# The first five attention steps of a banded-attention and FFN kernel: mask and maximum by one VectorE instruction per head pair, in place in the PSUM bank, and a new table of order constants for the beginning

## The chip, the cores and the metric

One NeuronCore of one Trainium2 chip runs the whole program. The metric is the device time of one execution in microseconds (us). Three timed runs of the kernel before gave 839.41, 840.69 and 839.26 us; the median is 839.41 us. Everything that is said of engines comes from one further, profiled execution.

## The reference

Attention over 8 sequences of 576 tokens with 8 heads of 64, each query seeing itself and the 63 keys ahead of it, and a feed-forward layer on the result. Cut to what matters:

```python
scores = scale * (q @ k.T)                       # scale = 1/8
mask = (rel >= 0) & (rel < 64)                   # rel = query position - key position
scores = where(mask, scores, -1e9)
attn = exp(scores - max(scores));  attn /= sum(attn) + 1e-9
x = (attn @ v)  as  [4608 tokens, 512]
h = x @ w_in                                     # 512 -> 2048
g = h if h >= 1;  0 if h <= -1;  (h + 1)**2 / 4 between
out = g @ w_out                                  # 2048 -> 512
```

All is float32. The kernel gets float32 accuracy out of a faster matmul format by splitting each operand into a high part (rounded to that format, `fp32r`) and a low part (the rest), and adding three products of parts.

## The kernel before

**Tiles and steps.** The tokens are cut into 9 tiles of 512, and an attention step handles 128 tokens of all 8 heads, so a tile takes four steps: 0 to 3 for tile 0, 4 to 7 for tile 1. Tiles 0, 1 and 2 go through the FFN plainly: for each of 16 slices f of the 2048 hidden columns, 12 matmuls of `ffn_in` (L1153, called IN below), the gate (`ffn_relu` L1163 on ACT, the square L1168 on ACT or L1170 on DVE, `ffn_gate` L1175 on DVE), the split into high and low (`ffn_high` L1180 on ACT, `ffn_low` L1185), and 12 matmuls of `ffn_out` (L1199, called OUT). In tile 0 the slices 0 to 2 go in two halves of 256 tokens (12 IN, 6 OUT each, f0h0 being the first half of slice 0). The last six tiles go in pairs by a scheme with fewer products (L928, L1014).

**Weights.** All weights are loaded once, as 64-bit integers that hold float32 values, and each slice is made into a high and a low part by seven operations: ACT `w_rest` (L342, tile u) and `w_sign` (L319, tile raw); DVE two limits (L323), a shift (L335) and `w_join` (L346); ACT `w_high` (L290, into wts); DVE `w_low` (L358). The slices 0 to 3 come in two units of 128x512 elements (8 units), the slices 4 to 15 in one of 128x1024.

**A step of attention.** `att_scores` (L439) multiplies q and k into two PSUM banks, one for each half of the heads. The steps 0 to 3 add the mask on PE: ahead of the scores, a matmul of an identity with a rounded mask (L432) is put into each bank; the identity and the mask are rounded by two ACT instructions (`round_masks`, L423 and L424). Then DVE takes the maximum over each row (L473), scales it (L475), ACT takes the exponentials out of the bank with their sums (L486, eight instructions a step), DVE inverts the sums (L493, L494) and multiplies (L501), PE transposes (L537), ACT or DVE copies the transposed block out (L290, L292, tile ptd), PE multiplies by v (L552), and the result is split into the high and low parts xh (L290 or L292) and xl (L565) that the FFN reads. Step 4 masks on DVE instead: L469 multiplies by the scale, adds the mask and writes sm in SBUF, L473 takes the maximum of it, and the exponentials read sm. From step 5 on (`s >= SOON`) another form is used: one DVE instruction per head, `tensor_tensor_reduce` (L462, two rows in the profile: CUSTOM_DVE and a short READ_ACCUMULATOR), adds the mask and takes the maximum, and a transposition through DRAM takes the place of PE's.

**What sets the order.** `Plan` (L128) is a list scheduler that runs while the program is built: each piece of work has a key, a cost for each engine that may take it, the pieces it depends on and the buffers it takes and gives back. It picks the next piece by when it could start and by its key. The engines' queues are then fixed, and each engine works its own queue in order and waits where an operand is not there. The constants at the head of the file (A_FIRST, W_FIRST, W_LATE, D_LATE, G_LATE and so on) are shifts of those keys. DMAs are issued from SP's queue in the plan's order too, but for the first k and the first unit of weights, which ACT's queue issues.

Of the kernel before, what the change touches and what calls it, by code (L numbers as in the profile page):

```python
# [20 lines left out]
P = 128  # L21
# [15 lines left out]
PE_MASKS = 4  # L37
# [15 lines left out]
V_LATE = 2.92  # L53
W0_KEY = -100.2
FIRST_LOAD = 0, (0,)
M_LATE = 1
W0_STEP = 12.29
FINE = 4
NWARM = 8
A_FIRST = (-102.6, -95.58, -95.43, -95)  # L60
A_NEXT = 1.57
A_STEP = 4.75
A_SPAN = 2.18
A_LEAD = 4.64
O_LAG = 2.79
# [33 lines left out]
V_LATE_2 = 14.69  # L99
# [119 lines left out]
def banded_attention_then_ffn(ctx: ExitStack, tc: tile.TileContext, q, k, v, w, masks, out, out_t, dims):  # L219
# [30 lines left out]
    idr = const.tile([P, P], F32R, name="idr")  # L250
    mskr = const.tile([P, 2, WIN], F32R, name="mskr")
# [170 lines left out]
    def round_masks():  # L422
        nc.scalar.copy(idr, idt)  # L423
        nc.scalar.mul(mskr, msk[:, :2], 1.0 / scale)  # L424

    def att_scores(s, masked, pool):
        qt, kt = qts.pop(s), kts.pop(s)
        banks = [banks_of_heads(pool) for _ in range(2)]
        if masked:
            m = mskr[:, variant(s), :].unsqueeze(1).broadcast_to([P, NP, WIN])  # L430
            for ps in banks:
                nc.tensor.matmul(ps.rearrange("p a n -> p (a n)"), lhsT=idr, rhs=m, start=True, stop=False)  # L432
        m, n = (SQ, NEAR) if near(s) else (QB, WIN)
        for p in range(NP):
            for i in range(SB // m):
                r = slice(i * m, (i + 1) * m)
                o = rows_of(i // 2, i % 2) if near(s) else r
                for h in range(2):
                    nc.tensor.matmul(  # L439
                        banks[h][o, p, :n], lhsT=qt[half[h], p, r], rhs=kt[half[h], p, i * m:i * m + n],  # L440
                        start=not masked, stop=not masked or p == NP - 1,
                    )
# [12 lines left out]
    def att_masked(s, h):  # L455
# [11 lines left out]
        m = nmsk[:, variant(s), :NEAR] if near(s) else msk[:, variant(s)]  # L467
        m = m.unsqueeze(1).broadcast_to(sm.shape)
        nc.vector.scalar_tensor_tensor(out=sm, in0=ps, scalar=scale, in1=m, op0=ALU.mult, op1=ALU.add)  # L469

    def att_max(s, h, masked):
        ps, sm, nm, _ = blk[s, h]
        nc.vector.tensor_reduce(out=nm, in_=ps if masked else sm, axis=AX.X, op=ALU.max, negate=True)  # L473
        if masked:
            nc.vector.tensor_scalar_mul(nm, nm, scale)  # L475

    def att_exp(s, h, masked):
# [190 lines left out]
    def add_step(t, i):  # L668
# [3 lines left out]
        masked = s < PE_MASKS  # L672
# [23 lines left out]
        needs = [xq, xk] + [last["r"]] * masked + last["s"]  # L696
        if before and (t < PLAIN or len(before) == BEHIND):
# [4 lines left out]
            def do(e):  # L702
                att_scores(s, masked, ps)
# [7 lines left out]
        else:  # L711
            xs = add(
                key, dict(PE=S_PE[near(s)] + 500 * masked), lambda e: att_scores(s, masked, ps), needs,
# [713 lines left out]
```

## Time and profile before

| | |
|---|---|
| three timed runs | 839.41, 840.69, 839.26 us |
| the profiled execution | 843.4 us |
| its span, from the first instruction to the last | 841.6 us |
| mean granted TensorE clock | 0.994 |
| PE busy | 821.6 us (98%) |
| DVE busy | 687.0 us (82%) |
| ACT busy | 533.5 us (63%) |
| POOL busy | 213.8 us (25%) |

The profiled execution took 1.8 us more than its span, and 4.0 us more than the median of the timed runs. In a list of groups, a row holds the line, engine, operation, output<-input, shapes and count, then busy time and mean duration in ns, then the idle time ahead of the group and what ended it. In a timeline a row is start, duration, engine, line and shapes, with the idle time ahead of it in brackets. Rows of one engine overlap: the next instruction starts a little before the row of the last one ends, so what an instruction costs in a full queue is the distance between starts. PE rows of small float32 matmuls come in twos per instruction (16 score matmuls are 32 records).

### The profile page before, as it was taken

What the parts mean: (1) busy time and instruction counts of PE and PEld (TensorE: products, weight loads), DVE (VectorE), ACT (ScalarE), POOL (GpSimd) and SP (SyncE); (2) the same over time, 40 slices, a digit from 0 to 9 for tenths busy, and PEclk for the clock granted to TensorE, in tenths of its full rate; (3) what the DMA queues carried; (4) which work ended last, traced back from release to release, by engine and by line L of the source; (5) the groups of instructions that cost most, each with busy time, mean ns of one, the idle gap of its engine ahead of it and who ended that gap; (6) DMA issues with size and microseconds to landing.
All of it is one profiled execution on the core that took longest, in us unless ns stands there. A gap on an engine that the chain in (4) does not pass through costs nothing.

```text
span 841.6 us, 18582 instructions
## 1 busy us (share of the span) xinstructions
PE 821.6 (98%) x6588; PEld 672.1 (80%) x6588; DVE 687.0 (82%) x1613; ACT 533.5 (63%) x1303; POOL 213.8 (25%) x226
## 2 busy tenths in 40 slices
PE   7889999999999999999999999999999999999998
PEld 5767788878787878788888888888888888888886
DVE  6999996468757789888899986888999848878964
ACT  5999983545654764756775654777756536566442
POOL 1000014335664636221233320122332201100100
PEclk8999999999999999999999999999999999999999
DMA  8994359996788797788898898888888877777775
GB/s 322 394 375 170 100 165 331 362 331 200 214 265 262 219 285 235 271 252 272 272 333 253 284 316 281 269 268 282 302 252 244 294 230 198 192 195 193 198 224 164
DMA packets 151901, 216.08 MB, mean 257 GB/s; under 512 B 11904, under 2 KB 75264, under 8 KB 151808
## 3 DMA queue, kind: packets, MB, share of 16 engines
q1 hardware_dynamic: 151520, 213.97, 80.2%
q8 instruction: 53, 0.87, 0.4%
q10 hardware_dynamic: 288, 0.92, 0.3%
q14 instruction: 40, 0.33, 0.1%
HBM read 163.72 MB, written 51.12 MB: 255 GB/s over the span
## 4 chain that ended last, share of the span: by engine, by line
PE 75%; DVE 10%; DMA 7%; ACT 3%; issue 2%; POOL 2%; SPq 1%; ACTq 0%; POOLq 0%; DVEq 0%
PE acc L1014 27%; PE ps_h L928 14%; PE acc L928 14%; PE ps_h L1153 8%; PE acc L1199 7%; DMA kept<-u 4%; PE ps_a L439 2%; DVE u L842 1%; PE ps_a L552 1%; DVE u L857 1%; PE ps_h L552 1%; DVE u L849 1%; DMA raw<-in_w 1%; DVE wts L358 1%; DMA kt<-in_k 1%
## 5 line engine op out<-in xcount | busy, mean ns | idle before, releaser
L1014 PE MATMUL acc<-op,wts 128*128 128x512 f32 x576 | 137.7, 390 | 0.0
L1153 PE MATMUL ps_h<-xh,wts 128*128 128x512 f32 (+1 forms) x424 | 131.2, 376 | 6.1 <-DVE a L1175 4.4
L290 ACT CAST op<-g 128x512 fp32r<-128x512 f32 x129 | 80.2, 622 | 77.4 <-PE acc L1014 49.3
L1014 PEld LDWEIGHTS acc<-op,wts 128*128 128x128 f32 x576 | 107.8, 188 | 22.5
L1199 PE MATMUL acc<-wts,gh 128*128 128x512 f32 x384 | 120.1, 394 | 0.7 <-ACT gh L1180 0.7
L482 ACT ACTIVATE sm<-sm,nm 128x96 f32<-128x96 f32 x248 | 89.5, 363 | 12.3 <-DVE nm L462 11.6
L1153 PEld LDWEIGHTS ps_h<-xh,wts 128*128 128x128 f32 x424 | 78.0, 190 | 22.6 <-DVE a L1175 6.5
L1005 DVE TENSOR_TENSOR op<-g,op 128x512 fp32r<-128x512 f32 x107 | 76.7, 718 | 20.7 <-ACT op L290 20.2
L928 PE MATMUL ps_h<-wts 128*128 128x512 f32 x360 | 92.0, 391 | 0.0
L928 PE MATMUL acc<-wts 128*128 128x512 f32 x360 | 91.5, 389 | 0.0
L1199 PEld LDWEIGHTS acc<-wts,gh 128*128 128x128 f32 x384 | 70.8, 188 | 16.0 <-ACT gh L1180 1.1
L1168 ACT ACTIVATE a<-a 128x512 f32<-128x512 f32 (+1 forms) x125 | 77.1, 617 | 3.8
L1153 PE MATMUL ps_h<-xl,wts 128*128 128x512 f32 (+1 forms) x212 | 78.8, 372 | 0.6 <-DVE xl L565 0.6
L928 PEld LDWEIGHTS acc<-wts 128*128 128x128 f32 x360 | 67.5, 188 | 14.2
L928 PEld LDWEIGHTS ps_h<-wts 128*128 128x128 f32 x360 | 67.2, 188 | 14.2
L1199 PE MATMUL acc<-wts,gl 128*128 128x512 f32 x192 | 75.3, 392 | 1.4 <-DVE gl L1185 1.4
L1163 ACT ACTIVATE a<-g 128x512 f32<-128x512 f32 x96 | 60.5, 630 | 19.4 <-DVE g L943 14.0
L1175 DVE SCALAR_TENSOR_TENSOR g<-a,g 128x512 f32<-128x512 f32 x96 | 68.1, 716 | 3.8 <-ACT a L1168 3.2
L1005 POOL TENSOR_TENSOR op<-g,op 128x512 fp32r<-128x512 f32 x28 | 36.1, 1295 | 129.5 <-ACT op L290 118.1
L1185 POOL TENSOR_TENSOR gl<-a,gh 128x512 fp32r<-128x512 f32 (+1 forms) x34 | 48.6, 1429 | 45.0 <-ACT gh L1180 43.2
L992 DVE TENSOR_TENSOR g<-g 128x512 f32<-128x512 f32 x83 | 58.4, 717 | 0.5
L1175 DVE SCALAR_TENSOR_TENSOR a<-a,ps_h 128x512 f32<-128x512 f32 (+1 forms) x53 | 33.3, 628 | 25.1 <-ACT a L1168 24.9
(145 smaller groups left out, 1544.5 us busy)
## 6 DMA issues: line engine op xcount, KB each, us to landing
wts<-kept SPq DMA_DIRECT2D x240, 256.0 KB, 3.6
vt<-in_v SPq DMA_DIRECT2D x72, 256.0 KB, 4.9
ptd<-moved SPq DMA_DIRECT2D x31, 512.0 KB, 4.7
kt<-in_k SPq DMA_DIRECT2D x35, 384.0 KB, 5.1
kept<-wts SPq DMA_DIRECT2D x48, 256.0 KB, 4.8
gh<-kept SPq DMA_DIRECT2D x48, 256.0 KB, 3.7
gl<-kept SPq DMA_DIRECT2D x48, 256.0 KB, 3.6
raw<-in_w SPq DMA_DIRECT2D x12, 1023.8 KB, 10.6
```

The lines of the kernel that those rows point to most:

```text
L290: nc.scalar.copy(dst, src)
L482: nc.scalar.activation(t, t, AF.Exp, bias=nm[:, g:g + 1], scale=-1.0, accum_out=den[:, g:g + 1])
L928: nc.tensor.matmul(ps, lhsT=r[:, part, cp], rhs=x_op(k, xp)[:, cp], start=j in (0, 1, 3, 4) and i == 0 and cp == 0, stop=j in (1, 2, 5, 6) ...
L992: engine[eng].tensor_tensor(out=g[:, out], in0=g[:, a], in1=g[:, b], op=op)
L1005: engine[eng].tensor_tensor(out=low, in0=g_of(n)[:, of], in1=high.bitcast(F32), op=ALU.subtract)
L1014: nc.tensor.matmul(opened[b][m], lhsT=r[:, part, m], rhs=op[xp], start=j in (0, 1, 3, 4) and i == 0 and n == 0, stop=j in (1, 2, 5, 6) and ...
L1153: nc.tensor.matmul(ps, lhsT=wts[f, 0][:, part, c * P:(c + 1) * P], rhs=x[:, c, r], start=(c == 0 and j == 0), stop=(c == NP - 1 and j == 2),)
L1163: nc.scalar.activation(gs[t, f, r.start][0], phs[t, f, r.start], AF.Relu, bias=0.5, scale=0.5)
L1168: nc.scalar.activation(a, a, AF.Square)
L1175: nc.vector.scalar_tensor_tensor(out=ps if t >= PLAIN else a, in0=a, scalar=1.0, in1=ps, op0=ALU.min, op1=ALU.max)
L1185: engine[eng].tensor_tensor(out=g[2], in0=g[0], in1=g[1].bitcast(F32), op=ALU.subtract)
L1199: nc.tensor.matmul(acc[t, i][:, n], lhsT=g[:, sub], rhs=wts[f, 1][:, part, n], start=(q == 0 and j == 0), stop=(q == NF - 1 and j == 2 and ...
```

## The change

The steps 0 to 4 now mask as the later steps do: for each of the four heads of a bank one `tensor_tensor_reduce` adds the mask to the negated, scaled scores, writes the result back into the bank where it stood, and leaves the minimum in nm. The exponentials read the bank (with scale -1), for step 4 too. The mask matmuls, `round_masks`, the two rounded tiles, the separate maximum and its scaling are gone. The rest of the diff is constants: those of the beginning (A_FIRST, the new A_SHIFT, W_FIRST with a value for each of 14 slices, W_LATE, D_LATE, L_LEAD_1, B_DUE_1, O_LAG_1 for tile 0) and, by small amounts, those of the later stages.

```diff
-PE_MASKS = 4
-A_FIRST = (-102.6, -95.58, -95.43, -95)
+A_FIRST = (-102.4, -117.29, -54.2, -100.65)
+A_SHIFT = (0.68, 0.08, 0.09, 3.56, 0.35, 0.89, -2.62, 0.86)
...
-    def round_masks():
-        nc.scalar.copy(idr, idt)
-        nc.scalar.mul(mskr, msk[:, :2], 1.0 / scale)
-
-    def att_scores(s, masked, pool):
+    def att_scores(s, pool):
         qt, kt = qts.pop(s), kts.pop(s)
         banks = [banks_of_heads(pool) for _ in range(2)]
-        if masked:
-            m = mskr[:, variant(s), :].unsqueeze(1).broadcast_to([P, NP, WIN])
-            for ps in banks:
-                nc.tensor.matmul(ps.rearrange("p a n -> p (a n)"), lhsT=idr, rhs=m, start=True, stop=False)
...
-        m = nmsk[:, variant(s), :NEAR] if near(s) else msk[:, variant(s)]
-        m = m.unsqueeze(1).broadcast_to(sm.shape)
-        nc.vector.scalar_tensor_tensor(out=sm, in0=ps, scalar=scale, in1=m, op0=ALU.mult, op1=ALU.add)
-
-    def att_max(s, h, masked):
-        ps, sm, nm, _ = blk[s, h]
-        nc.vector.tensor_reduce(out=nm, in_=ps if masked else sm, axis=AX.X, op=ALU.max, negate=True)
-        if masked:
-            nc.vector.tensor_scalar_mul(nm, nm, scale)
+        nm = blk[s, h][2]
+        for p in range(NP):
+            nc.vector.tensor_tensor_reduce(
+                out=ps[:, p], in0=ps[:, p], in1=msk[:, variant(s)], scale=-scale,
+                scalar=3.0e38, op0=ALU.add, op1=ALU.min, accum_out=nm[:, p:p + 1],
+            )
...
         for p in range(NP):
             nc.scalar.activation(
-                sm[:, p, :], (ps if masked else sm)[:, p, :], AF.Exp, bias=nm[:, p:p + 1],
-                scale=scale if masked else 1.0, accum_out=den[:, p:p + 1],
+                sm[:, p, :], ps[:, p, :], AF.Exp, bias=nm[:, p:p + 1], scale=-1.0, accum_out=den[:, p:p + 1],
             )
```

What moves is seen best in the queues. ACT's queue from its first compute instruction on, before: u, raw and wts are the three weight operations, `sm,den` the exponentials of steps 0 (out of ps_a) and 1 (out of acc), ptd a transposed block that is copied out.

```order
6 L342 ACTIVATE u<-raw 128x512
7 L319 ACTIVATE raw<-raw 128x512
8 L486 ACTIVATE sm,den<-ps_a,nm 128x128 x8
9 L290 CAST wts<-u 128x512
10 L342 ACTIVATE u<-raw 128x512
11 L290 COPY ptd<-ps_h 128x512
12 L486 ACTIVATE sm,den<-acc,nm 128x128 x8
13 L319 ACTIVATE raw<-raw 128x512
14 L342 ACTIVATE u<-raw 128x512
15 L319 ACTIVATE raw<-raw 128x512
16 L290 CAST xh<-acc 128x4x128
```

The same stretch of ACT's queue now (lines are shifted by the edit: L341, L318 and L289 are the weight operations, L474 the exponentials).

```order
4 L341 ACTIVATE u<-raw 128x512
5 L318 ACTIVATE raw<-raw 128x512
6 L341 ACTIVATE u<-raw 128x512
7 L318 ACTIVATE raw<-raw 128x512
8 L289 CAST wts<-u 128x512 x2
9 L341 ACTIVATE u<-raw 128x512
10 L318 ACTIVATE raw<-raw 128x512
11 L341 ACTIVATE u<-raw 128x512
12 L289 CAST wts<-u 128x512
13 L318 ACTIVATE raw<-raw 128x512
14 L474 ACTIVATE sm,den<-ps_a,nm 128x128 x8
15 L474 ACTIVATE sm,den<-acc,nm 128x128 x8
```

Four units of weights now stand ahead of the first exponential where one stood; ahead of the first gate (row 22 before, row 29 now) stand six first and second weight operations in place of three, five third ones in place of two, and two xh in place of one, while the exponentials of the steps 0 to 3 and the copies there are the same. SP's queue follows: it now begins with a unit of weights and has six of them ahead of the q of step 2, where it had one.

PE's queue before, from the scores of step 0 on: L432 are the mask matmuls, L439 scores, L537 transposes, L552 the products with v.

```order
2 L432 MATMUL ps_a<-mskr,idr 128x512 x2
3 L439 MATMUL ps_a<-kt,qt 64x128 x16
4 L432 MATMUL acc<-mskr,idr 128x512 x2
5 L439 MATMUL acc<-kt,qt 64x128 x16
6 L537 MATMUL ps_h<-idt,sm 128x128 x8
7 L432 MATMUL ps_a<-mskr,idr 128x512 x2
8 L439 MATMUL ps_a<-kt,qt 64x128 x16
9 L552 MATMUL acc<-ptd,vt 64x64 x16
10 L537 MATMUL ps_h<-idt,sm 128x128 x8
11 L432 MATMUL acc<-mskr,idr 128x512 x2
12 L439 MATMUL acc<-kt,qt 64x128 x16
13 L552 MATMUL acc<-ptd,vt 64x64 x16
```

PE's queue now, up to the first FFN matmul (L430 scores, L524 transposes, L539 the products with v, L1133 IN).

```order
2 L430 MATMUL ps_a<-kt,qt 64x128 x16
3 L430 MATMUL acc<-kt,qt 64x128 x16
4 L524 MATMUL ps_h<-idt,sm 128x128 x12
5 L539 MATMUL acc<-ptd,vt 64x64 x16
6 L524 MATMUL ps_h<-idt,sm 128x128 x4
7 L430 MATMUL ps_a<-kt,qt 64x128 x16
8 L539 MATMUL acc<-ptd,vt 64x64 x16
9 L430 MATMUL acc<-kt,qt 64x128 x16
10 L1133 MATMUL ps_h<-xh,wts 128x256
```

The eight mask matmuls are gone. Behind these rows, before, come 12 IN (f0h0), then the transposes and products with v of the steps 2 and 3, then 12 IN, 6 OUT, 36 IN, 6 OUT, 12 IN, the scores of step 4, 12 IN of slice 3, 6 OUT, the scores of step 5, 30 OUT, 12 IN (slice 4), 4 transposes, 24 IN (slices 5 and 6), 4 transposes, 12 OUT. Now come 24 IN (f0h0 and f1h0) ahead of the transposes of the steps 2 and 3, then 12 IN, 12 OUT, the scores of step 4, 24 IN, 6 OUT, 12 IN, 12 IN of slice 3, 12 OUT, 12 IN (slice 4), 6 OUT, 4 transposes, 12 IN (slice 5), 24 OUT, the scores of step 5, 12 IN (slice 6), 4 transposes. Both lists hold the same matmuls.

On DVE the work for the first three units of weights, but for one subtraction, stands ahead of the first mask instruction, and eight `tensor_tensor_reduce` a step stand where two maxima and two scalings stood. DVE's queue is also what releases PE in that stretch: its copy of a transposed block of step 2 (row 107) waits for transposes that PE's queue has behind those 24 IN.

More of the change, by code (lines that the diff above doesn't have):

```diff
@@ L52 @@
 K_LOAD = 1040
-V_LATE = 2.92
-W0_KEY = -100.2
+V_LATE = 26.14
+W0_KEY = -126.82
 FIRST_LOAD = 0, (0,)
-M_LATE = 1
-W0_STEP = 12.29
+M_LATE = -16.15
+W0_STEP = 22.65
 FINE = 4
 NWARM = 8
-A_FIRST = (-102.6, -95.58, -95.43, -95)
[L61 to L65, printed above, removed]
+A_FIRST = (-102.4, -117.29, -54.2, -100.65)
+A_SHIFT = (0.68, 0.08, 0.09, 3.56, 0.35, 0.89, -2.62, 0.86)
+A_NEXT = -2.55
+A_STEP = 7.86
+A_SPAN = 71.21
+A_LEAD = -14.41
+O_LAG = 3.01
+O_LAG_1 = 5.63
 O_LAG_DMA = 2300
@@ L440, in att_scores @@
                         banks[h][o, p, :n], lhsT=qt[half[h], p, r], rhs=kt[half[h], p, i * m:i * m + n],
-                        start=not masked, stop=not masked or p == NP - 1,
+                        start=True, stop=True,
                     )
@@ L681, in add_step @@
             key = a_keys[s]
-            due = min(key + A_SPAN, soon(s))
-        lk = key - L_LEAD
+            due = min(key + A_SPAN, soon(s)) + A_SHIFT[s]
+        lk = key - (L_LEAD if s >= JOIN else L_LEAD_1)
         apart = A_SUPER[t > PLAIN][1]
-        if s == 0:
-            last["r"] = add(lk, dict(ACT=480), lambda e: round_masks())
         if s == PE_STEPS - 2:
@@ L695, in add_step @@
         last["v"] = [xw]
-        needs = [xq, xk] + [last["r"]] * masked + last["s"]
+        needs = [xq, xk] + last["s"]
         if before and (t < PLAIN or len(before) == BEHIND):
@@ L712, in add_step @@
             xs = add(
[L713 removed]
+                key, dict(PE=S_PE[near(s)]), lambda e: att_scores(s, ps), needs,
                 takes=[ps, ps, "sm"], gives=[("qt", xq), ("kt", xk)],
@@ L719, in add_step @@
             for h in range(2):
-                x = xs
-                if not masked:
-                    x = add(due + D_LATE[0], dict(DVE=MASKED[near(s)]), lambda e, h=h: att_masked(s, h), [x, last["m"]] if near(s) else [x], gives=[(ps, xs, h)])
-                x = add(due + D_LATE[1], dict(DVE=800 if masked else MAXIMUM[near(s)]), lambda e, h=h: att_max(s, h, masked), [x])
-                x = add(
-                    due + D_LATE[2], dict(ACT=1375 if masked else EXP[near(s)]), lambda e, h=h: att_exp(s, h, masked), [x],
-                    gives=[(ps, xs, h)] * masked,
-                )
+                x = add(due + D_LATE[0], dict(DVE=820), lambda e, h=h: att_masked(s, h), [xs])
+                x = add(due + D_LATE[2], dict(ACT=EXP[0]), lambda e, h=h: att_exp(s, h), [x], gives=[(ps, xs, h)])
                 x = add(due + D_LATE[3], dict(DVE=420), lambda e, h=h: att_inverse(s, h), [x])
@@ L1205, in out_late @@
         if t < PLAIN - 1 or q < NF - 2:
-            return O_LAG
+            return O_LAG if t else O_LAG_1
         return O_CHANGE[0] if q == NF - 2 else O_CHANGE[1 + i // 2]
```

65 lines of the change are left out of this document (32 added, 33 removed).

## The prediction

> **What bounds the kernel now.** I read the busy time by stage first, since the share over the whole span hides where time is lost. Columns: stretch, its length, then busy time of PE, PEld, DVE, ACT and POOL, then the granted TensorE clock.
>
> ```profile
> 20.00:30.00 10.00, 7.74 (x93) 6.76 (x91) 8.63 (x26) 9.39 (x40) 0.00 (x0) 0.83 1.02 368
> ...
> 50.00:60.00 10.00, 7.86 (x91) 5.00 (x89) 9.90 (x27) 9.91 (x22) 0.00 (x0) 1.00 0.98 352
> ...
> 70.00:187.00 117.00, 116.45 (x992) 95.33 (x990) 90.82 (x209) 80.19 (x170) 24.73 (x26) 1.00 0.74 236
> 187.00:346.00 159.00, 155.25 (x1580) 125.54 (x1585) 125.38 (x385) 96.35 (x291) 91.18 (x104) 1.00 0.79 236
> 346.00:835.00 489.00, 489.00 (x3450) 402.25 (x3440) 409.80 (x866) 297.61 (x679) 94.94 (x82) 1.00 0.82 255
> ```
>
> From 346 us on PE is never idle, and from 70 to 346 it loses 0.55 + 3.75 = 4.3 us. So nearly all that can be won or lost lies ahead of 70 us, where DVE and ACT are nearly full (8.63 and 9.39 of ten, then 9.90 and 9.91) and PE is not: they prepare weights, attention and gates, and PE waits for what they deliver. The waits say the same; each row is who waited for whom, us in total, times, longest.
>
> ```profile
> PE ps_h L1153 <- DVE a L1175: 4.4, 6, 1.6
> PE ps_h L537 <- DVE den L493: 1.7, 1, 1.7
> PE ps_h L1153 <- DVE xh L292: 1.7, 1, 1.7
> PE acc L439 <- DMA kt<-in_k: 1.6, 1, 1.6
> ```
>
> A change of the beginning is therefore worth what it does to one date: when PE has done a given list of matmuls after which it stays busy. As that milestone I take the start of step 4's products with v. Behind it before lie the 120 IN of slices 0 to 6, 60 OUT, the scores of the steps 0 to 5, the products with v of 0 to 3. In the new queue the same list ends behind the four transposes that follow slice 6's IN.
>
> ```profile
> 74.76 1.15 PE L552 MATMUL ps_a<-ptd,vt 128*64 128x64 f32 x32
> ```
>
> So the milestone now is 74.76 us.
>
> **The change, part by part.** *Mask matmuls.* Eight go, with two ACT instructions.
>
> ```profile
> L432 PE MATMUL ps_a<-mskr,idr 128*128 128x512 f32 x4 | 2.4, 701 | 0.0
> ...
> 4.89 1.20 PE L432 MATMUL ps_a<-mskr,idr 128*128 128x512 f32 x2
> ```
>
> They stand where PE waits for loads or for ACT: step 0's mask runs at 4.89 us, three us before the first weights are there, and step 1 then still waits the 1.6 us for k. So I take their removal at nothing on the path; at most it is worth the 2.4 us of the row of steps 0 and 2, if the scores of step 2 were on the path.
>
> *DVE's work.* Rows of DVE's timeline: a maximum of a half of step 0 and that of the next half, step 4's mask and maximum, and two masks of the later kind that follow each other.
>
> ```profile
> 7.23 0.69 DVE L473 TENSOR_REDUCE nm<-ps_a 128x4 f32<-128x512 f32 x1 [4.74 <-PE ps_a L439]
> ...
> 8.03 0.68 DVE L473 TENSOR_REDUCE nm<-ps_a 128x4 f32<-128x512 f32 x1
> ...
> 47.41 1.27 DVE L469 SCALAR_TENSOR_TENSOR sm<-ps_a,msk 128x512 f32<-128x512 f32 x2
> ...
> 49.20 1.26 DVE L473 TENSOR_REDUCE nm<-sm 128x4 f32<-128x512 f32 x2
> ...
> 54.36 0.25 DVE L462 CUSTOM_DVE_ANT_0 sm<-ps_a,nmsk 128x96 f32<-128x96 f32 x1
> ...
> 54.54 0.25 DVE L462 CUSTOM_DVE_ANT_0 sm<-ps_a,nmsk 128x96 f32<-128x96 f32 x1
> ```
>
> A maximum with its scaling takes 8.03 - 7.23 = 0.80 us a half, 1.6 a step; step 4 takes 1.27 + 1.26 = 2.53. The new instruction comes, on 96 columns, 0.18 us apart; 128 columns, and the result written into PSUM, which no row shows, lie between 0.18 and 0.24 (a third more). I take 0.21, so 1.7 us a step: four steps cost 0.1 us more each, step 4 gains 0.8, in all 0.4 us less DVE work; with 0.18 or 0.24 for 0.21 it is 1.7 less or 0.7 more. [...]
>
> *The beginning on ACT.* ACT starts as the first unit of weights lands.
>
> ```profile
> 7.73 0.66 ACT L342 ACTIVATE u<-raw 128x512 uint32<-128x512 uint32 x1 [3.62 <-DMA raw<-in_w]
> ...
> 28.70 0.38 ACT L1163 ACTIVATE a<-ps_h 128x256 f32<-128x256 f32 x1
> ...
> 39.43 0.62 ACT L290 CAST wts<-u 128x512 fp32r<-128x512 f32 x1
> 39.95 0.38 ACT L1163 ACTIVATE a<-ps_h 128x256 f32<-128x256 f32 x1
> ...
> 40.86 0.66 ACT L342 ACTIVATE u<-raw 128x512 uint32<-128x512 uint32 x1
> 41.43 0.39 ACT L1180 CAST gh<-a 128x256 fp32r<-128x256 f32 x1
> ...
> 20.86 0.57 ACT L290 CAST xh<-acc 128x512 fp32r<-128x512 f32 x1
> ```
>
> As much is queued about that load as now (512 KB of weights take the place of q and v), so I keep 7.73. The first gate is at 28.70 now. Ahead of it stand three more first operations and three more third ones: by distances between starts 0.57 (41.43 - 40.86) and 0.52 us (39.95 - 39.43); the second I price as the first. With one more xh (0.5) that is 3 x (0.57 + 0.57 + 0.52) + 0.5 = 5.5 us, so 34.2 us, and about 1 us of waits that the order has and the present one hasn't: DVE's join is waited for three times in the first eight weight operations with nothing else queued. I take 35.2. So the FFN's first gate comes 6.5 us later, with three units of weights more already done.
>
> *PE from there.* The first 24 IN stand in a stretch that follows a nearly idle PE. Rows of PE's timeline; the last one is of the chain that ended last (start, duration, work).
>
> ```profile
> 26.25 0.39 PE L1153 MATMUL ps_h<-xl,wts 128*128 128x256 f32 x1 [0.56 <-DVE xl L565]
> ...
> 28.46 2.39 PE L537 MATMUL ps_a<-idt,sm 128*128 128x128 f32 x12
> ...
> 38.02 0.40 PE L1153 MATMUL ps_h<-xh,wts 128*128 128x256 f32 x2
> ...
> 38.38 0.40 PE L1153 MATMUL ps_h<-xh,wts 128*128 128x256 f32 x2
> ...
> 45.87 1.10 PE L439 MATMUL ps_a<-kt,qt 64*64 64x128 f32 x32
> 46.90 0.50 PE L1153 MATMUL ps_h<-xh,wts 128*128 128x512 f32 x1
> ...
> 65.07 0.60 PE L537 MATMUL ps_a<-idt,sm 128*128 128x128 f32 x4
> 65.42 0.48 PE L1153 MATMUL ps_h<-xh,wts 128*128 128x512 f32 x1
> ...
> 84.30 2.72 PE ps_h L1153 x12
> ```
>
> The first block of IN runs at (28.46 - 26.25) / 11 = 0.20 us a matmul, a later one at 0.12 (three matmuls, one of them in a row left out, in 38.38 - 38.02). So the 24 take 2.9 to 4.8 us; I take 4, nearer to the slow row, whose place is the same. DVE's copy of step 2's transposed block, behind them, comes up to 1.9 us later, with all that DVE has queued there; the waits below cover that. [...]
>
> Behind 35.2 ACT has twelve instructions up to the high part of f1h0, of which I estimate 0.45 each by the distances above (half are of 256 columns), 5.4 us. DVE's low part of it with one subtraction of weights ahead is 1.1 more, and six OUT are 1.4 (half of 2.72). So PE ends the first 12 OUT at 43.1. From there the list holds: scores 1.03 (46.90 - 45.87) and 1.0, 36 IN of 256 at 0.12 = 4.3, 48 IN of 512 and 48 OUT at 2.72 a dozen = 21.8, eight transposes 0.7 (65.42 - 65.07 for four). Together 28.8 us, so the milestone is at 71.9 if nothing is waited for.
>
> Whether it waits is read from three rows, the last ACT operation on slice 6's weights and two stretches after it:
>
> ```profile
> 65.46 1.04 ACT L290 CAST wts<-u 128x1024 fp32r<-128x1024 f32 x1
> ...
> 80.00:100.00 20.00, 20.00 (x175) 16.12 (x175) 19.69 (x44) 17.92 (x36) 0.00 (x0) 1.00 0.34 115
> 100.00:120.00 20.00, 20.00 (x234) 15.89 (x233) 19.90 (x60) 19.69 (x46) 0.00 (x0) 1.00 0.40 126
> ```
>
> PE needs slice 6's weights some 3 us before the milestone, and their last ACT operation is at 65.46 now; in the new queue ACT has nearly the same work ahead of it (0.7 us more). At 66.2, with 1.04 us for the cast and as long or twice as long for DVE's subtraction, the weights are ready at 68.3 to 69.3; PE wants them at about 69: no room. And DVE stays full until 120, so PE, being earlier, has none later either. Waits that the present queue has not, the late copy above all, cost between 0 and 3 us (1.9 for the slow IN, 1 for the weights); I allow 1, since part of the copy's delay falls where ACT still works off exponentials: milestone 72.9, against 74.76, so 1.9 us earlier.
>
> *The rest.* The later constants move by tenths. They touch the 4.3 us of waits between 70 and 346 us. The costliest:
>
> ```profile
> 312.86 0.50 PE L1153 MATMUL ps_h<-xh,wts 128*128 128x512 f32 x1 [1.63 <-DVE a L1175]
> ...
> 310.91 0.42 DVE L842 TENSOR_TENSOR u<-wts 128x256 f32<-128x256 f32 x1 [2.59 <-DMA kept<-u]
> ...
> DVE u L842 <- DMA kept<-u: 15.2, 9, 2.9
> ```
>
> DVE waits for a store that frees a buffer, and the gate that PE needs is queued behind it. The new queue has the same kind of instructions in other places; I take the sum as unchanged, between 2.2 less (half of it) and 2 more.
>
> **The sum.** 843.4 us of the profiled execution less 1.9 gives 841.5. That execution stands 4.0 us above the median of the timed runs, so on the median 839.41 - 1.9 = 837.5.
>
> **The rivals.** *DVE as the bound, slower.* With the cover gone, DVE's idle time in the first 45 us goes straight into PE. DVE was idle 1.4 us of the ten from 20 to 30 alone; the new order has DVE stand for transposes behind the 24 slow IN, for exponentials of two steps in a row, and for joins' sources. The new order is slower once they come to 2.9 us (1 allowed and 1.9 of gain). Two more waits of the 1.7 us of the list above, and 40 mask instructions at 0.24 and not 0.21 (1.2 us), are 4.6 us more than I allow: 837.5 + 4.6 = 842.1. For it: DVE at 9.9 of 10, and no spare until 120 us. Against it: three units of weights are done before the first gate. Chance 0.23.
>
> *The gain is given back between 70 and 346.* DVE's store waits are fixed by DMA, not by PE; a PE that comes 1.9 us earlier waits 1.9 us longer at the same stores: 839.4. For it: all of the 4.3 us are waits of this kind or for gates. Against it: from 70 to 187 they were 0.55. Chance 0.20.
>
> *More is won.* The beginning runs without the allowed waits (milestone 71.9, 2.9 us) and half of the later 4.3 goes: 839.41 - 2.9 - 2.1 = 834.4. For it: DVE has 0.4 us less to do. Against it: there is no room at slice 6. Chance 0.14.
>
> **Chances.** My case has 0.43 and runs from 836.5 to 838.5 (waits of 0 to 2 us). Repeated medians of this kernel tell about 0.2% (1.7 us) from no change, at 837.7. So the case is 0.27 faster and 0.16 the same; more won is faster (0.14); given back is 0.06 faster, 0.11 the same and 0.03 slower; the slower rival is 0.20 slower and 0.03 the same. Faster 0.47, same 0.30, slower 0.23. The range goes from 833.2 (the 834.4 less half of the masks' upper price of 2.4) to 842.1.
>
> **What would show it.** In the new profile the first gate (L1143 on ACT) at 34 to 36 us; the 24 IN at 0.2 us first and 0.12 later; the mask row about 0.21 us apart; step 4's products with v, or the end of slice 6's four transposes, at 72 to 74 us; waits of PE between there and 346 of 2 to 6 us. The prediction is wrong if the milestone is past 74.8, if PE waits for weights between 70 and 125 us, or if the waits after 70 are past 6.

## The result, and the profile after

The changed kernel takes 847.44 us, the median of four runs (846.96 to 849.37), against 839.84 for four of the kernel before: a ratio of 1.0094, with a 95% interval of 1.0075 to 1.0113. Its profiled execution took 849.37 us (span 847.4), 6.0 more than the first profiled execution of before. The forecast was 837.5 in a range up to 842.1, so it was wrong in sign and outside its range.

Busy time by stage of the changed kernel, in the columns of the first fence of the prediction:

```profile
20.00:30.00 10.00, 4.74 (x45) 4.10 (x45) 9.40 (x40) 8.15 (x34) 0.00 (x0) 1.00 0.53 217
50.00:60.00 10.00, 9.47 (x86) 8.01 (x85) 9.73 (x34) 8.47 (x15) 0.00 (x0) 1.00 0.94 353
70.00:187.00 117.00, 117.00 (x968) 96.01 (x967) 90.91 (x223) 84.95 (x192) 22.76 (x29) 1.00 0.75 242
187.00:346.00 159.00, 156.29 (x1607) 126.97 (x1606) 121.70 (x373) 98.60 (x287) 79.00 (x92) 1.00 0.79 239
346.00:835.00 489.00, 487.89 (x3513) 400.88 (x3494) 411.77 (x882) 300.89 (x696) 100.50 (x87) 1.00 0.83 257
```

From 70 us on PE loses 2.71 + 1.11 = 3.8 us, about the 4.3 of the first profiled execution of before. The loss lies ahead of 70 us: between 20 and 30 us PE works 4.74 us of ten and DVE 9.40. PE's waits say whom it stands for (us in total, times, longest):

```profile
PE ps_h L524 <- DVE sm L488: 9.8, 1, 9.8
PE ps_a L430 <- DMA raw<-in_w: 6.5, 1, 6.5
PE ps_h L1133 <- DVE xl L552: 1.9, 1, 1.9
PE ps_a L539 <- DMA ptd<-moved: 1.6, 1, 1.6
...
PE ps_a L524 <- DVE den L480: 1.0, 1, 1.0
```

Its timeline at the dates that the prediction named: the first full block of IN, step 3's transposes, step 4's scores (the first 12 OUT are done there), a wait for a gate, and slice 6's transposes, whose end, 80.78, is the milestone.

```profile
36.52 0.39 PE L1133 MATMUL ps_h<-xl,wts 128*128 128x256 f32 x1 [1.87 <-DVE xl L552]
...
43.00 0.63 PE L524 MATMUL ps_a<-idt,sm 128*128 128x128 f32 x4 [1.04 <-DVE den L480]
...
50.69 1.10 PE L430 MATMUL ps_a<-kt,qt 64*64 64x128 f32 x32
...
56.79 0.39 PE L1133 MATMUL ps_h<-xh,wts 128*128 128x256 f32 x1 [0.53 <-DVE a L1155]
...
80.43 0.60 PE L524 MATMUL ps_a<-idt,sm 128*128 128x128 f32 x4
```

The milestone was forecast at 72.9: it is 7.9 us late, and that is the whole miss of 9.9 us (847.44 - 837.5) but for 2 us. This one execution stands 1.9 us above the median of its kernel. On ACT's timeline stand the first weights, three waits for joins, a fourth, and the first gate:

```profile
8.65 0.66 ACT L341 ACTIVATE u<-raw 128x512 uint32<-128x512 uint32 x1 [5.71 <-DMA raw<-in_w]
...
11.79 0.62 ACT L289 CAST wts<-u 128x512 fp32r<-128x512 f32 x1 [0.54 <-DVE u L345]
...
13.93 0.62 ACT L289 CAST wts<-u 128x512 fp32r<-128x512 f32 x1 [1.53 <-DVE u L345]
...
17.66 0.62 ACT L289 CAST wts<-u 128x512 fp32r<-128x512 f32 x1 [1.29 <-DVE u L345]
...
33.10 0.62 ACT L289 CAST wts<-u 128x512 fp32r<-128x512 f32 x1 [1.13 <-DVE u L345]
...
40.80 0.39 ACT L1143 ACTIVATE a<-ps_h 128x256 f32<-128x256 f32 x1
```

And on DVE's timeline, the mask instruction with its second row, the read of the accumulator. The starts are 0.39 us apart inside a bank (17.46, 17.85) and 0.21 where the next bank begins (18.64, 18.85):

```profile
17.46 0.30 DVE L460 CUSTOM_DVE_ANT_0 ps_a<-ps_a,msk 128x128 f32<-128x128 f32 x1
17.67 0.15 DVE L460 DVE_READ_ACCUMULATOR2_ANT nm<- 128x1 f32 x1
17.85 0.30 DVE L460 CUSTOM_DVE_ANT_0 ps_a<-ps_a,msk 128x128 f32<-128x128 f32 x1
...
18.64 0.30 DVE L460 CUSTOM_DVE_ANT_0 ps_a<-ps_a,msk 128x128 f32<-128x128 f32 x1
18.85 0.14 DVE L460 DVE_READ_ACCUMULATOR2_ANT nm<- 128x1 f32 x1
18.85 0.33 DVE L460 CUSTOM_DVE_ANT_0 ps_a<-ps_a,msk 128x128 f32<-128x128 f32 x1
```

The eight of a step end at 20.28, so a step costs 2.82 us where 1.7 was forecast. The program's list of instructions shows what stands between them: in a bank each waits for a semaphore of DVE's own, the first of a bank only for PE.

```
24 L460 ISA ps_a,nm<-ps_a,msk 128x128 [waits PE_49]
25 L460 ISA nm 128x1
26 L460 ISA ps_a,nm<-ps_a,msk 128x128 [waits DVE_49]
27 L460 ISA nm 128x1
28 L460 ISA ps_a,nm<-ps_a,msk 128x128 [waits DVE_49]
```

### The profile page after: what moved, and what is told of

It is laid out like the page before. It is cut to its first block, busy times and chain, and to the rows that moved or that the text cites. A ratio compares the mean times of both kernels' runs of the same rounds, so it can differ in the third digit from the quotient of the medians.

```text
span 847.4 us, 18605 instructions
## 1 busy us (share of the span) xinstructions
PE 818.5 (97%) x6580; PEld 672.8 (79%) x6580; DVE 684.4 (81%) x1664; ACT 537.3 (63%) x1313; POOL 205.2 (24%) x223
## 4 chain that ended last, share of the span: by engine, by line
PE 58%; DVE 1%; DMA 0%; ACT 0%; issue 0%; POOL 0%; SPq 0%; ACTq 0%; POOLq 0%
PE acc L994 27%; PE acc L908 14%; PE ps_h L908 14%; PE ps_a L430 2%; PE acc L539 1%; PE ps_h L539 1%; PE ps_a L539 1%; DMA vt<-in_v 0%; DVE u L837 0%; DVE wts L610 0%; ACT o L289 0%; DVE u L1013 0%; DVE u L822 0%; DVE sm L453 0%; DVE u L829 0%
## 5 line engine op out<-in xcount | busy, mean ns | idle before, releaser
L1133 PE MATMUL ps_h<-xh,wts 128*128 128x512 f32 (+1 forms) x424 | 130.6, 376 | 0.6 <-DVE a L1155 0.5
L289 ACT CAST op<-g 128x512 fp32r<-128x512 f32 x128 | 79.6, 622 | 73.2 <-PE acc L994 41.7
L985 DVE TENSOR_TENSOR op<-g,op 128x512 fp32r<-128x512 f32 x113 | 80.9, 718 | 26.5 <-ACT op L289 26.0
L1133 PEld LDWEIGHTS ps_h<-xh,wts 128*128 128x128 f32 x424 | 78.3, 191 | 15.9 <-DVE a L1155 1.2
L1148 ACT ACTIVATE a<-a 128x512 f32<-128x512 f32 (+1 forms) x128 | 79.2, 619 | 3.8
L1133 PE MATMUL ps_h<-xl,wts 128*128 128x512 f32 (+1 forms) x212 | 79.0, 373 | 1.9 <-DVE xl L552 1.9
L1155 DVE SCALAR_TENSOR_TENSOR g<-a,g 128x512 f32<-128x512 f32 x96 | 71.0, 747 | 3.9 <-ACT a L1148 3.2
L972 POOL TENSOR_TENSOR g<-g 128x512 f32<-128x512 f32 x21 | 27.2, 1293 | 135.0 <-DVE op L985 57.6
L1165 POOL TENSOR_TENSOR gl<-a,gh 128x512 fp32r<-128x512 f32 (+1 forms) x34 | 43.9, 1292 | 58.7 <-ACT gh L1160 55.5
L453 DVE CUSTOM_DVE_ANT_0 sm<-ps_a,nmsk 128x96 f32<-128x96 f32 x248 | 47.1, 249 | 5.6 <-PE ps_a L430 5.6
```

Of the source, the lines that this page charges most:

```text
L289: nc.scalar.copy(dst, src)
L453: nc.vector.tensor_tensor_reduce(out=sm[:, :, g], in0=ps[:, p].rearrange("p (c n) -> p c n", n=SQ), in1=m, scale=-scale, scalar=3.0e38, op ...
L985: engine[eng].tensor_tensor(out=low, in0=g_of(n)[:, of], in1=high.bitcast(F32), op=ALU.subtract)
L1133: nc.tensor.matmul(ps, lhsT=wts[f, 0][:, part, c * P:(c + 1) * P], rhs=x[:, c, r], start=(c == 0 and j == 0), stop=(c == NP - 1 and j == 2),)
L1148: nc.scalar.activation(a, a, AF.Square)
L1155: nc.vector.scalar_tensor_tensor(out=ps if t >= PLAIN else a, in0=a, scalar=1.0, in1=ps, op0=ALU.min, op1=ALU.max)
```

## The experiments

Two theories: the in-place instruction with its wait is the loss (theory 1 of the first four runs), or the order is, which puts weights ahead of attention. All ratios are to the kernel before.

**The instruction and the order apart.** Writing to SBUF, in the changed order:

```diff
-                out=ps[:, p], in0=ps[:, p], in1=msk[:, variant(s)], scale=-scale,
+                out=sm[:, p], in0=ps[:, p], in1=msk[:, variant(s)], scale=-scale,
-                sm[:, p, :], ps[:, p, :], AF.Exp, ...
+                sm[:, p, :], sm[:, p, :], AF.Exp, ...
```

> The order of the changed kernel is kept on every engine; only the place that the mask instruction writes is another: SBUF (tile sm) and not in place in the bank, and the exponential reads it there. In the trace of the changed kernel eight of these instructions take 2.82 us a step (17.46 to 20.28), 0.39 apart inside a bank and 0.21 where the bank changes; in the program each one behind the first of a bank waits for the one before it, since both touch the same tile in PSUM. Theory 1 (the price of the in-place instruction is the loss): the waits are gone, the instructions come 0.21 us apart, 1.7 us a step, 1.1 us less in each of four steps; the first gate comes 3 to 4 us earlier and the time is 843.5 to 845. Theory 2 (the order is the loss, with weights ahead of attention): also 0.21 apart, but the time is regained by less than 1.5 us, 846 to 847.5. Theory 3 (a 128-column instruction on a bank is slow wherever it writes): still 0.35 to 0.39 apart, 847.4.

844.49 us, ratio 1.0042 (1.0025 to 1.0058). DVE's mask instructions, the first gate and slice 6's transposes:

```profile
17.47 0.28 DVE L460 CUSTOM_DVE_ANT_0 sm<-ps_a,msk 128x128 f32<-128x128 f32 x1
17.68 0.08 DVE L460 DVE_READ_ACCUMULATOR2_ANT nm<- 128x1 f32 x1
17.68 0.28 DVE L460 CUSTOM_DVE_ANT_0 sm<-ps_a,msk 128x128 f32<-128x128 f32 x1
...
39.40 0.36 ACT L1143 ACTIVATE a<-ps_h 128x256 f32<-128x256 f32 x1
...
76.34 0.60 PE L524 MATMUL ps_a<-idt,sm 128*128 128x128 f32 x4
```

They come 0.21 us apart, and the milestone is at 76.69, 4.1 us earlier. In the times 0.52 of the 0.94% are gone: theory 1 holds for about half of the loss. Only 1.4 us of it shows at the gate, where 3 to 4 were expected. The rest comes behind it, where the steps 2 to 4 keep DVE: step 3's transposes waited 1.04 us for an inverted sum, and the gate that PE stood for at 56.79 was queued behind step 4's eight instructions.

The second run keeps the result in the bank and takes the banks in turn:

```diff
-        nm = blk[s, h][2]
-        for p in range(NP):
+        for p in range(h * NP // 2, (h + 1) * NP // 2):
+            for i in range(2):
+                ps, _, nm, _ = blk[s, i]
```

> The order of the changed kernel, still in place in the banks, but the eight instructions of a step go over the two banks in turn, so that each waits for the last but one. Theory 1 (the wait for the one before is the price): 0.21 to 0.25 us apart, 1.7 to 2.0 us a step; the time is near that of the run that writes to SBUF, within 1 us, 843.5 to 846. Rival (writing into PSUM is slow by itself): still 0.35 to 0.39 apart, 2.8 us a step, and the time stays at 847.4 or goes past it, since the first half is ready later.

1.0046 (1.0029 to 1.0063), milestone 76.43, and the instructions, in DVE's timeline, come 0.25 us apart:

```profile
17.68 0.33 DVE L461 CUSTOM_DVE_ANT_0 ps_a<-ps_a,msk 128x128 f32<-128x128 f32 x1
17.93 0.14 DVE L461 DVE_READ_ACCUMULATOR2_ANT nm<- 128x1 f32 x1
17.93 0.33 DVE L461 CUSTOM_DVE_ANT_0 ps_a<-ps_a,msk 128x128 f32<-128x128 f32 x1
```

So of the 0.18 us between 0.39 and 0.21, the wait for the one just before makes 0.14. The other 0.04 is seen where an instruction that writes PSUM starts together with the accumulator read of the last one: its row is 0.33 us, and its own read starts 0.25 us after it (17.68, 17.93), against 0.21 for the one that writes to SBUF.

The third run has the order of before with the new operations in steps 0 to 3, the fourth the new order with the operations of before there:

```diff
 # third: the kernel before, beside the removal of the mask matmuls and of the rounding
-        nc.vector.tensor_reduce(out=nm, in_=ps if masked else sm, axis=AX.X, op=ALU.max, negate=True)
-        if masked:
-            nc.vector.tensor_scalar_mul(nm, nm, scale)
+        if masked:
+            for p in range(NP):
+                nc.vector.tensor_tensor_reduce(out=ps[:, p], in0=ps[:, p], ...)
+            return
 # fourth: the changed kernel, beside the mask matmuls and the rounding put back for steps 0 to 3
+        if s < 4:
+            nc.vector.tensor_reduce(out=nm, in_=ps, axis=AX.X, op=ALU.max, negate=True)
+            nc.vector.tensor_scalar_mul(nm, nm, scale)
+            return
```

> The kernel before, with its constants and its order on every engine; only the operations of steps 0 to 3 are the new ones (mask and maximum by the in-place instruction, no mask matmuls, no rounding of the masks on ACT). Theory 1 (the price of the in-place instruction is the loss): DVE gets 2.8 us a step for 1.6, four times 1.2 us on a DVE that is nearly full: 3 to 5 us slower than before, 843 to 845. Theory 2 (the order is the loss): 839.5 to 841.5, as the old order hides it. If it comes out below 839.4, the removal of the mask matmuls is worth more than nothing.

1.0038 (1.0024 to 1.0052), milestone 76.36.

> The changed kernel with its constants and its order; only steps 0 to 3 have the operations of the kernel before (mask matmul into the bank, maximum from the bank with a scaling, two rounding instructions ahead of everything on ACT); step 4 stays as changed. Theory 1 (the price of the in-place instruction is the loss): maxima of 1.6 us a step for 2.8, so 843 to 845, about as the run that writes to SBUF. Theory 2 (the order is the loss): 846 to 848.5.

1.0028 (1.0016 to 1.0041), milestone 75.68. So each part alone costs time, 0.3 to 0.4%, and together they cost 0.94%: neither theory is enough.

**The kernel before once more.**

> The kernel before, unchanged, profiled once more. Its first profiled execution took 843.4 us, 3 to 4 us more than the median of its timed runs, while the changed kernel's stands only 1.9 above its own. If that execution was a typical one with a profiler's cost, this one too takes 843 to 844 and its fourth-step products with v start at 74.5 to 75; if it was a slow one, this one takes 840 to 842, and the trace shows where the 2 us were.

It took 839.73 us: the first profiled execution was a long one. Its milestone and a stretch of later work:

```profile
73.67 1.15 PE L552 MATMUL ps_a<-ptd,vt 128*64 128x64 f32 x32
```

```profile
187.00:346.00 159.00, 157.95 (x1613) 127.95 (x1612) 127.30 (x396) 99.38 (x305) 91.30 (x102) 1.00 0.80 242
```

The milestone is 1.1 us earlier than in the first, and PE loses 1.05 us in 187 to 346, not 3.75. The sum of the prediction stood on that first execution.

The order of before with the mask instruction writing to SBUF (the third run's edit with `out=sm[:, p]`):

> The order of the kernel before, with the mask instruction in steps 0 to 3 writing to SBUF, and no mask matmuls. Before it stood the same with the instruction in place: 1.0038 of before. Theory (the wait for the one before it in the bank is the price): 1.7 us a step for 2.8, so of those 3.2 us nearly all come back, ratio 0.998 to 1.002; DVE has then the same work as before within 0.4 us, ACT 0.3 us more a step for exponentials from SBUF (0.385 apart for 0.345). Below 0.998 the removal of the mask matmuls is worth something on the path after all; above 1.002 the new operations cost more than the trace of the queue says.

1.0022 (1.0012 to 1.0032), milestone 74.71. The waits cost 1.65 us here (76.36 to 74.71) and 4.1 in the new order. Even without them the new operations win nothing in the order of before: the ratio is just past the 0.998 to 1.002 that was expected, and no run separates what makes the rest.

**What in the order.** These runs move single pieces of work behind others in the plan's written order. They start from the run that writes to SBUF, but for those of which another operation is said; their lines stand 20 to 60 higher than in the changed kernel.

```diff
+EDITS = (
+    ('load_q 0', 'w_load (0, (1,))'),
+    ('load_q 1', 'w_load (1, (0,))'),
+)
```

> The run that writes to SBUF in the new order, with one thing changed: the loads of q for step 0 and step 1 change places on SP, so step 0's comes at 1.2 us and not behind two units of weights and step 1's at 3.4. Theory 1 (the order of DVE's and ACT's queues is the loss): step 0's scores start 3 to 4 us earlier (7.5 to 8.5 for 11.7), and the time stays within 1 us of 844.5, since their mask instructions stand behind three joins on DVE (17.5 us) whatever PE does. Rival (late data is the loss): 2 us or more faster, below 842.5.

1.0045 (1.0029 to 1.0061). Step 0's scores start at 8.15 us, not 11.68, and next to nothing follows (gate 38.92, milestone 76.22, each 0.5 us earlier, at about the same ratio): the 6.5 us for which PE stood there were hidden by DVE's queue.

```diff
...
+    ('att_masked 0 0', 'w_join (0, (0,))'), ('att_masked 0 1', 'att_masked 0 0'),
+    ('att_exp 0 0', 'w_high (0, (0,))'), ('att_exp 0 1', 'att_exp 0 0'),
+    ('att_masked 1 0', 'w_join (0, (1,))'), ('att_masked 1 1', 'att_masked 1 0'),
+    ('att_exp 1 0', 'w_sign (1, (0,))'), ('att_exp 1 1', 'att_exp 1 0'),
```

> As the run with the two loads exchanged, and beside it the mask instructions and exponentials of steps 0 and 1 are moved up among the first three units of weights on DVE and ACT (step 0 behind the first unit's join, step 1 behind the second's); the same instructions, nothing else moved. Theory 1 (ACT stands 5.5 us for joins since nothing else is queued between a unit's operations): the waits of 1.51, 1.28 and 0.55 us at 11.8 to 17.7 us go, the first gate comes 2 to 3 us earlier (36.4 to 37.4 for 39.4), and the time is 841 to 842.7. Rival (the loss lies behind the first gate, or in the loads of later weights): the gate comes earlier, but PE waits as much more later, 843.5 to 845.

1.0048 (1.0033 to 1.0063): a miss. ACT's waits for the joins of the second and third units are gone, but the timeline of DVE and ACT shows where the time went:

```profile
21.55 0.69 DVE L389 TENSOR_TENSOR wts<-u,wts 128x512 fp32r<-128x512 f32 x1 [2.25 <-ACT wts L321]
...
24.86 0.58 ACT L321 COPY ptd<-ps_h 128x512 f32<-128x512 f32 x1 [2.77 <-PE ps_h L556]
...
38.36 0.36 ACT L1175 ACTIVATE a<-ps_h 128x256 f32<-128x256 f32 x1
```

DVE stands for an ACT cast that the edit had made late, step 0's normalizing is queued behind it, PE's transposes behind that, and ACT's copy of them behind PE. The next run moves what was behind:

```diff
+    ('att_inverse 0 0', 'w_low (0, (1,))'), ('att_inverse 0 1', 'att_inverse 0 0'),
+    ('att_normalize 0 0', 'att_inverse 0 1'), ('att_normalize 0 1', 'att_normalize 0 0'),
...
+    ('att_transposed 0 0', 'w_rest (1, (1,))'), ('att_transposed 0 1', 'att_transposed 0 0'),
+    ('att_inverse 1 0', 'w_join (1, (0,))'), ('att_normalize 1 0', 'att_inverse 1 0'),
+    ('att_inverse 1 1', 'w_low (1, (0,))'), ('att_normalize 1 1', 'att_inverse 1 1'),
```

> The last run but this one, attention among the weights, won 0.6 us at the first gate (38.36 for 38.92) where 2 to 3 were expected: ACT's three waits for joins went, but DVE stood 2.25 us for an ACT cast with the normalizing of step 0 queued behind it, and ACT then 2.77 us for the transposes behind that. Here that normalizing goes ahead of the third unit's operations on DVE, step 1's behind its join, and step 0's two copies on ACT ahead of the third cast; nothing else. Theory 1 (waits in the queues ahead of the first gate are the loss of the new order): the 2.25 and 2.77 us go, the first gate comes at 35.9 to 37, slice 6's transposes end at 73.2 to 74.5, and the time falls by 1 to 2.5 us, to ratios of 1.002 to 1.0035. Rival (PE is not held by that gate, or the waits move on again): gate and transposes move by less than 1 us and the ratio stays at 1.004 to 1.005.

1.0018 (1.0008 to 1.0029). The waits on ACT's timeline and the milestone, 73.78:

```profile
23.36 0.67 ACT L385 ACTIVATE u<-raw 128x512 uint32<-128x512 uint32 x1 [0.18 <-DVE wts L401]
...
26.02 0.62 ACT L333 CAST wts<-u 128x512 fp32r<-128x512 f32 x1 [0.81 <-DVE u L389]
...
36.47 0.36 ACT L1187 ACTIVATE a<-ps_h 128x256 f32<-128x256 f32 x1
...
73.42 0.60 PE L568 MATMUL ps_a<-idt,sm 128*128 128x128 f32 x4
```

From the run with the loads exchanged, the two edits bring the gate 2.4 us earlier (38.92 to 36.47) and the milestone as much (76.22 to 73.78): queue waits ahead of the gate were most of the order's loss (1.0045 to 1.0018).

The next two runs move loads on SP's queue. The first of them has the operations of the kernel before in the steps 0 to 3, the second the new ones, into SBUF.

```diff
+    ('load_masks', 'load_k 2'), ('w_load (1, (0,))', 'load_q 1'),
```

> The order of the next run (attention among the weights, no queue behind the cast, masks' load late), with the operations of the kernel before in steps 0 to 3: mask matmuls and maxima from the bank. With the operations before, the changed order stood at 1.0028 of before. Theory 1: the same 1.5 to 3 us come off as with the new operations, ratio 0.999 to 1.001, that is as the kernel before; if the old operations are as good as the new in this order, both have the same ratio within 0.001. Rival: 1.002 to 1.003, the order gives nothing back.

1.0008 (0.9997 to 1.0018), milestone 73.86.

> As the run without the queue behind the cast, and on SP the load of the later masks (144 KB, wanted by step 5 alone) goes behind the loads of steps 2 and 3, and step 1's q ahead of the second unit's first half. In the new order the first weights land at 8.5 to 8.7 us, in the old at 7.5 to 7.8, with these 144 KB and 256 KB of q and 512 KB of weights issued ahead of 3.5 us. Theory (the share of the DMA queues is what makes the first weights late): ACT starts at 7.6 to 8.1 and the first gate comes 0.4 to 0.9 us earlier than without it; the time falls by as much, near what a run can tell. Rival (the first unit is late by itself): ACT starts at 8.5 again.

1.0009 (0.9998 to 1.0019), milestone 73.87. The first weights still land at 8.69 us, and the gate is where it was (36.57): the rival holds. The operations of before have their gate 1.15 us earlier (35.42) and the same milestone.

**The rest.** The new instruction in place with the banks in turn, and on ACT step 0's conversion ahead of a cast; then also the first q ahead of the second half of the first weights:

```diff
+    ('att_high', 'att_transposed 1 0'),
+    ('w_load (0, (1,))', 'load_q 0'),
```

> All mends together: attention among the weights, no queue behind the cast, masks' load late, and the mask instruction in place with the banks in turn (0.25 us apart, exponentials from the bank 0.345 apart) in place of SBUF (0.21, and 0.385 from SBUF); step 0's first conversion for the FFN goes ahead of the cast that ACT waits 0.81 us for. Theory 1 (each us ahead of the first gate is a us of the kernel): ACT has 32 times 0.04 = 1.3 us less, and up to 0.8 of waits; DVE 0.3 us a step more. The first gate comes at 34.8 to 35.8 (36.57 without), slice 6's transposes end at 72.2 to 73.2 (73.87), and the ratio falls from 1.0009 to 0.998 to 1.0000. Rival (the rest is not on ACT any more): gate later than 36.2 or time unchanged, 1.0005 to 1.0015.

1.0022 (1.0013 to 1.0032): a miss, the gate came later, at 37.05. With the banks in turn, the first half's last minimum comes with the seventh of eight instructions, and ACT's exponentials wait for it:

```profile
13.61 0.37 ACT L522 ACTIVATE sm<-ps_a,nm 128x128 f32<-128x128 f32 x1 [1.19 <-DVE nm L508]
```

> As the run with all mends, and on SP step 0's q goes ahead of the first unit's second half of weights, which is issued at 1.2 and not at 0.74 us. Moving the masks' load did not make the first weights land earlier (8.69 us). Theory (the second half, 512 KB issued 0.4 us ahead of the first on another queue, shares the engines with it): the first half lands at 7.6 to 8.2, and the gate comes up to 0.8 us earlier, ratio 0.997 to 0.9995. Rival (the bytes issued in the first 4 us are what counts): within 0.2 us of 8.6, and no change.

1.0017 (1.0007 to 1.0027). The first weights land at 8.20, the gate comes at 36.56, 0.5 earlier. The ratio stays as it was within the intervals, and far from the 0.997 to 0.9995 of the theory. The last two have both of these edits without the banks in turn, with the operations of before and with the new ones into SBUF:

> The mended order with the operations of the kernel before in steps 0 to 3 (mask matmuls, maxima from the bank), with the two further mends of the last runs that are free of the banks in turn: step 0's first conversion ahead of the cast that ACT waits 0.80 us for, and step 0's q ahead of the second half of the first weights. Without these two: gate at 35.42 us, transposes' end 73.86, ratio 1.0008. Theory (each us ahead of the first gate is a us of the kernel): the gate comes 0.8 to 1.2 us earlier, at 34.2 to 34.7, the transposes end at 72.7 to 73.2, ratio 0.9993 to 1.0000. Rival (what is left between this order and the one before lies behind the gate): gate earlier, ratio 1.0005 to 1.0012.

1.0013 (1.0001 to 1.0025), gate 34.60, milestone 73.06.

> The same order as the run beside it, with the new instruction writing to SBUF in steps 0 to 4. Without the two mends: gate at 36.57 us, transposes' end 73.87, ratio 1.0009. Theory: gate at 35.3 to 35.9, transposes' end 72.7 to 73.3, ratio 0.9993 to 1.0002. If it stands over the run beside it by more than 0.0005, the new operations cost time even without their waits (0.04 us more for each exponential from SBUF, 32 of them); if it stands below, taking the mask matmuls and two ACT instructions away is worth something.

1.0004 (0.9996 to 1.0013). The first weights, the gate and the transposes (end 72.88):

```profile
7.75 0.66 ACT L389 ACTIVATE u<-raw 128x512 uint32<-128x512 uint32 x1 [4.79 <-DMA raw<-in_w]
...
35.57 0.36 ACT L1191 ACTIVATE a<-ps_h 128x256 f32<-128x256 f32 x1
...
72.53 0.60 PE L572 MATMUL ps_a<-idt,sm 128*128 128x128 f32 x4
```

Gates and milestones came where they were expected, 0.8 to 1.0 us earlier than in the runs without these edits. The times did not follow clearly: one ratio rose (1.0008 to 1.0013), the other fell (1.0009 to 1.0004), and both lie above the theory's ranges (up to 1.0000 and 1.0002). No version beats the kernel before.

## Why the prediction was wrong, point by point

| kernel | gate | milestone | ratio |
|---|---|---|---|
| before, second execution | 27.82 | 73.67 | 1 |
| forecast | 35.2 | 72.9 | 0.9977 |
| changed | 40.80 | 80.78 | 1.0094 |
| into SBUF | 39.40 | 76.69 | 1.0042 |
| and queue waits mended | 36.47 | 73.78 | 1.0018 |
| and first weights, one more cast | 35.57 | 72.88 | 1.0004 |

The milestone as the date that counts was right: over the runs it and the ratio go together, to about 2 us in the worst case (milestone 75.65 with 1.0048 against 75.68 with 1.0028). With three terms set near what the forecast had assumed, it comes out at 72.88. That it agrees to 0.02 is luck: the gate is 0.4 us later than forecast, and the way from there to the milestone as much shorter (37.3 for 37.7). A milestone varies by 1.1 us between two executions of one kernel, so single steps below are good to about 1 us.

**"I take 0.21, so 1.7 us a step" failed,** and so did its bounds of 0.18 to 0.24: 4.1 of the 7.9 us, if this step is mended first (in the order of before the same waits cost 1.65 us, so the split depends on the order). The rows that it took came from instructions that write another tile than they read. In place, each waits for the one before. The wait stands in the program and could have been read there. "Step 4 gains 0.8" became 0.3 lost (2.82 for 2.53). Into SBUF the same instruction came 0.21 us apart, so the row had the price right for the case that it came from, an instruction that writes another tile; the kernel had another case.

**"About 1 us of waits that the order has" failed:** 2.9 us. The prediction saw that ACT waits for joins "with nothing else queued" and counted them as 1 us. ACT's waits from the first weights up to the gate are 7.5 us in the changed kernel, 5.5 into SBUF and 2.0 in the last run; they were 2.7 and 1.7 in the two executions of before. The run that moved only attention up won little, since waits moved to the next in the queue; two edits together gave the 2.4 us of gate, and the exchanged loads 0.5 us, which is inside the scatter.

**"So I keep 7.73" for the first weights failed** by 0.9 us, although about as many bytes are issued around that load: 8.53 to 8.74 in the runs with the second half of the unit issued 0.4 us ahead of the first, 7.75 to 8.20 in the three with q ahead of it. Late masks changed nothing. This and one cast are the last 0.9 us of the milestone, which the times do not show.

**The base was 1.1 us too late.** The gain of 1.9 us was taken from the milestone 74.76 of one execution; against 73.67 the forecast's 72.9 is 0.8 us. The last run has that milestone, and its ratio allows a gain of 0.04%, 0.3 us, at most. PE's idle time from 70 to 835 us is 2.4 us in that execution of before and 3.5 in the last run, which would give the gain back. But over all traces it goes from 1.8 to 4.3 in the order of before (four) and from 2.1 to 4.2 in the new one (thirteen), so it may be scatter. This stays open, and with it the rival by which the gain is given back; no run changed the later constants alone. The three steps and the base, 7.9 and 1.1 us, make 846.5 of the 847.44 measured.

**Right** were three points. Removing the mask matmuls was taken at nothing: the pairs that differ in the operations alone stand at 1.0008 and 1.0009, 1.0013 and 1.0004, with intervals that overlap. These pairs exchange all the operations, so it is the exchange as a whole that is worth nothing clear of scatter; no run takes the matmuls away alone. From the first 12 OUT to the milestone 29.8 were forecast, and 30.1 came (50.69 to 80.78). The waits behind 70 us stayed under 6. From the gate to those OUT 7.9 were forecast: 8.0 in the run with the mended queues, 9.9 in the changed kernel, where DVE's masks were late.

**The 24 IN were luck.** They took 4 us as forecast (23 of them from 36.52 to 40.55), but the forecast had 0.20 us a matmul first and 0.12 later, and the changed kernel has it the other way round. That the slow ones come first was an estimate from the place of the slow row. PE had worked on attention almost without a pause from 25.26 to 34.65, and the granted clock was 1.00 from 36.5 to 37.8 us and 0.50 from 38.0 to 40.5:

```profile
36.74 0.40 PE L1133 MATMUL ps_h<-xh,wts 128*128 128x256 f32 x2
36.98 0.28 PE L1133 MATMUL ps_h<-xl,wts 128*128 128x256 f32 x1
...
39.03 0.63 PE L1133 MATMUL ps_h<-xh,wts 128*128 128x256 f32 x2
39.45 0.41 PE L1133 MATMUL ps_h<-xl,wts 128*128 128x256 f32 x1
```

In the last run the same stretch ran at 0.12 throughout (23 from 30.68 to 33.73). A sum that comes out with its parts exchanged does not bear out the slow start that it was made from.

**The slower rival** named the mechanism, DVE without cover in the first 45 us and the mask instruction's price, and was priced by the same bound of 0.24: it ended at 842.1. At 0.35 a piece (2.82 / 8) and 2.9 us of queue waits it comes to 837.5 + 40 x 0.14 + 2.9 = 846.0.

## What to carry to other kernels

Take an instruction's price from a row with the same dependence on its neighbours, not only the same shape: a loop that reads and writes one tile can wait for itself at every turn (here 0.39 us apart in place, 0.21 into another tile), and the program's waits show that before a run does. When an order puts one unit's chain across two engines back to back, count the whole chain of the other engine as a wait for each unit, since mending one such wait can show the next in the queue (here 2.25 us on DVE and 2.77 on ACT, once two of ACT's waits for joins were gone). And take the base of a sum from more than one execution, when the gain is of the size by which executions differ (here 1.1 us of milestone).

## What the runs showed of the hardware

A wait for the instruction just before, on the same engine, cost 0.14 to 0.18 us here: 0.39 us apart against 0.25 and 0.21. In the changed kernel, with the wait, the next mask instruction starts 0.03 us behind the end of the accumulator read of the last one (17.82, 17.85); in the run that writes to SBUF, without it, together with that read (17.68).

PE ran at little over half of its later rate where the record shows the full clock. In the changed kernel the same 16 score matmuls took 1.99 us and later 1.10, and the granted clock is 1.00 from 10 to 20 us, and also from 11.5 to 14.0 alone. What slowed the first ones, the runs do not show:

```profile
11.79 1.99 PE L430 MATMUL ps_a<-kt,qt 64*64 64x128 f32 x32 [6.54 <-DMA raw<-in_w]
...
31.02 1.10 PE L430 MATMUL ps_a<-kt,qt 64*64 64x128 f32 x32
```

```profile
10.00:20.00 10.00, 3.69 (x64) 3.32 (x64) 8.20 (x28) 6.32 (x14) 0.00 (x0) 1.00 1.04 414
```

Exponentials of 128x128 came 0.385 us apart out of SBUF (18.75 to 21.83 for eight steps, in the run that writes there) and 0.35 out of PSUM (19.09 to 21.55 for seven, in the changed kernel), so the mask instruction that is cheaper for DVE is dearer for ACT.
